# Float64 weights as twice their float32 by an integer addition, its steps spread over nine units of the attention

## The chip, the cores and the metric

The kernel runs on one core of one Trainium2 chip. The metric is the device time of one execution in microseconds (us). The core has TensorE (PE, its weight loads PEld), VectorE (DVE), ScalarE (ACT), GpSimd (POOL) and SyncE (SP, which here only issues DMAs). Each engine works off its own queue in order, so an instruction that waits holds back all that stand behind it on that engine.

## What is computed

```python
x = attention(q, k, v)          # 2 x 8 heads, 576 tokens, 64 wide, rotary; -> 1152 x 512
h = x @ w_in                    # w_in 512 x 2048, float64
x = (h / (1 + exp(-h))) @ w_out # w_out 2048 x 512, float64
out = 0
for e in range(4):              # w1[e] 512 x 1024, w2[e] 1024 x 512, float32
    out += p[:, e:e+1] * (relu(x @ w1[e]) @ w2[e])
```

q, k, v, w1 and w2 are float32. `w_in` and `w_out` come as float64, and no engine reads float64: each word is seen as two 32-bit integers, the low half `lw` and the high half `hw`, and must be turned into float32 on the chip. All large products are made with a high and a low part of each operand (`wh` and `wl` for weights: `wh` is the weight rounded to TensorE's fp32r, `wl` the rest), three matmuls for each product.

## The kernel before, in words

The attention works on 8 pairs of heads, each pair in 9 **units** (`P.units`: a block of 128 query rows of one head; the ninth takes the last 64 rows of both heads). `allu` holds the 72 units; the loop `for i, (P, un)` runs over them, `s = i % 9` is the unit's place in its pair. A unit's scores (`s`, L402 and on) go to PSUM, VectorE takes the row maximum (`nm`, L421), ScalarE the exponential (`p`, L431), TensorE transposes `p` into PSUM (L307), ScalarE copies the high part out (`pth`, L469) and VectorE the low part (`ptl`, L474), and later units multiply these by V (`b`, L507). `tmp` and `xu` (L517, L519) put the two halves of such a product together, `xn` (L560) normalizes, and `xh`, `xl` (L555, L556) are its split on ScalarE and GpSimd. The strings `ORDER` give the order of these steps inside each unit by hand, the lists `PLAN` the extra work of a unit; GpSimd rotates the next pair's keys and queries (L236 to L273) and splits its V (L290).

The conversion of the float64 weights is spread between them. `widen` (L83) makes the steps for one slice of 512 columns; a class `Feed` holds slices that wait, and `feed.tick(i in CONV)` at the end of every unit first runs one step of each slice under way and then, if the unit is in `CONV`, starts another, which issues its load (`raw0`, L1029, on SP) at once. In the attention four slices (unit 0 of `units`) are converted, with the steps of `slow=True`: four units in a row. They start at units 15, 24, 33 and 51 (later entries find nothing to start, but for 69). The other 28 slices (three steps each) are converted behind the attention, during the product with `w_in` and `w_out` (L645 to L675), while TensorE works; then come the experts (`l1r`, `Quartet`, `l2b`). One slice takes, before:

```python
ACT  t  = |hw| as float32                          # L90
DVE  lw = lw >> 9;  lw = hw << 23 | lw             # L91, L94
DVE  t  = max(t, 2**-15);  t = t << 3 & 0x3FFFF000 # L97, L100
DVE  t  = hw & 0xC0000000 | t                      # L103
ACT  wh = t                                        # L106
DVE  hw = t & 0xFF800000;  wl = lw * 2**-43 * hw   # L109, L112
```

Of the kernel before, what the change touches and what calls it, by code (L numbers as in the profile page):

```python
# [7 lines left out]
F32 = mybir.dt.float32  # L8
F32R = mybir.dt.float32r
U32 = mybir.dt.uint32  # L10
AF = mybir.ActivationFunctionType
ALU = mybir.AluOpType
# [5 lines left out]
ORDER = ['TvHSMEXVBL', 'SvTEBHVXML', 'vSTHEVMXBL', 'vSEVTBMXHL', 'THEvSVXMBL', 'vSVETHXMBL', 'vVSTEHMLXB', 'vTHSXLBEMV', 'vTSEXHVMBL']  # L18
ORDER0 = ['ETSHXMvVBL', 'TSEHXvVMBL', 'TSEHXMvVBL', 'TSXvEHMVBL', 'TXvVESHMBL', 'SEXVMTvHBL', 'SXMvVTEHLB', 'XESvMTVHBL', 'STvXEMHVBL']
ORDER2 = ['vSTEHLXVMB', 'vTVHSEXLMB', 'SvVEXTHMLB', 'vSEXMTHBVL', 'vTSVEXHMLB', 'vEVSTMXHBL', 'VETvSXHMLB', 'TvSVHEXMLB', 'vSMVTXEBHL']  # L20
CONV = [15, 24, 33, 51, 58, 61, 69]
DELAY = 2
RB1 = 0
RB0 = 4
# [7 lines left out]
def f32(ap):  # L32
    return ap.bitcast(F32)
# [3 lines left out]
def fused_kernel(ctx, tc, q, k, v, w_in, w_out, dprobs, w1, w2, cst, out):  # L37
    nc = tc.nc
# [7 lines left out]
    pers = ctx.enter_context(tc.tile_pool(name="pers", bufs=1))  # L46
# [16 lines left out]
    def new_slot(pool, i):  # L63
        wslot[i] = (
            pool.tile([128, FT, 512], F32R, name=f"wh{i}"),
            pool.tile([128, FT, 512], F32R, name=f"wl{i}"),
        )

    new_slot(pers, 0)

    w_in = w_in.bitcast(U32).rearrange("d (f a) -> d f a", a=2)
    w_out = w_out.bitcast(U32).rearrange("f (d a) -> f d a", a=2)
# [10 lines left out]
    def widen(cv, raw, wh, wl, slow=False):  # L83
        lw, hw = (raw.rearrange("p (n a) -> p n a", a=2)[:, :, a] for a in range(2))
        T = {}
        V = nc.vector

        def t0():
            T["t"] = t = cv.tile([128, 512], U32, name="cvt")
            nc.scalar.activation(f32(t), f32(hw), AF.Abs)  # L90
            V.tensor_scalar(lw, lw, 9, None, ALU.logical_shift_right)  # L91

        def t1():
            V.scalar_tensor_tensor(lw, hw, 23, lw, ALU.logical_shift_left, ALU.bitwise_or)  # L94

        def t2():
            V.tensor_scalar(f32(T["t"]), f32(T["t"]), 2.0 ** -15, None, ALU.max)  # L97

        def t3():
            V.tensor_scalar(T["t"][:], T["t"][:], 3, 0x3FFFF000, ALU.logical_shift_left, ALU.bitwise_and)  # L100

        def t4():
            V.scalar_tensor_tensor(T["t"][:], hw, 0xC0000000, T["t"][:], ALU.bitwise_and, ALU.bitwise_or)  # L103

        def t5():
            nc.scalar.copy(wh, f32(T["t"]))  # L106

        def t6():
            V.tensor_scalar(hw, T["t"][:], 0xFF800000, None, ALU.bitwise_and)  # L109

        def t7():
            V.scalar_tensor_tensor(wl, lw, 2.0 ** -43, f32(hw), ALU.mult, ALU.mult)  # L112

        def together(*fns):
            return lambda: [fn() for fn in fns]

        if slow:
            return [together(t0, t1), together(t2, t3, t4), t5, together(t6, t7)]
        return [together(t0, t1), together(t2, t3, t4), together(t5, t6, t7)]

    class Feed:
        def __init__(self):
# [46 lines left out]
    def bank(n, tag="b"):  # L169
        t = ps1.tile([128, 512], F32, tag=tag, name=tag)  # L170
        return t[:, 0:n]
# [422 lines left out]
    def flush(items):  # L594
        todo = list(items)
        items.clear()
        for e in todo:
            e()
# [27 lines left out]
    def mbank():  # L626
        psM.append(psM.pop(0))
        return psM[-1].tile([128, 512], F32, name="m")
# [3 lines left out]
    def l1(c, f, nb):  # L632
        if nb == 0:
            gt[c, f] = (
                gp.tile([128, NT], F32R, name="gh"),
                gp.tile([128, NT], F32R, name="gl"),
            )
        gh, gl = gt[c, f]
        wh, wl = wslot[(2 * c) % 4]
        ps = mbank()  # L640
        o = ps[:, 0:NB]
        cols = slice(nb * NB, (nb + 1) * NB)
        fs = slice(f * 128, (f + 1) * 128)
        for d in range(4):
            nc.tensor.matmul(o, wh[:, d, fs], xh[d][:, cols], start=(d == 0), stop=False)  # L645
            nc.tensor.matmul(o, wh[:, d, fs], xl[d][:, cols], start=False, stop=False)  # L646
            nc.tensor.matmul(o, wl[:, d, fs], xh[d][:, cols], start=False, stop=(d == 3))  # L647
        hi, lo = gh[:, cols], gl[:, cols]
        th = ep.tile([128, NB], F32, name="th")
        g2 = ep.tile([128, NB], F32, name="g2")  # L650
        nc.scalar.activation(th[:], o, AF.Tanh, scale=0.5)
        nc.vector.scalar_tensor_tensor(g2[:], th[:], 1.0, o, ALU.add, ALU.mult)
        flush(held)

        def split():
            nc.scalar.copy(hi, g2[:])  # L656
            (nc.gpsimd if c and nb < 2 else nc.vector).tensor_tensor(lo, g2[:], f32(hi), ALU.subtract)  # L657

        held.append(split)
# [20 lines left out]
    def xsplit(src, dst, cols):  # L680

        hi, lo = (t[cols] for t in dst)
        return [lambda: nc.scalar.activation(hi, src, AF.Copy, scale=0.5),
                lambda: nc.vector.scalar_tensor_tensor(lo, src, 0.5, f32(hi), ALU.mult, ALU.subtract)]

    def xforms(j):

# [38 lines left out]
    def wforms(raw):  # L726

        q = {x: raw[:, 2 * dh:2 * dh + 2, 256 * fh:256 * fh + 256]
             for x, dh, fh in (("a", 0, 0), ("b", 1, 0), ("c", 0, 1), ("d", 1, 1))}
        T = {}  # L730

        def task(name, add=None):
            hi, lo = wf[name]

            def s0():
                if add:
                    x, y, op = add
                    T[name] = cv.tile([128, 512], U32, name="cvt")
                    t = f32(T[name]).rearrange("p (k f) -> p k f", k=2)
                    nc.vector.tensor_tensor(t, src(x), src(y), op)  # L740
                nc.scalar.copy(hi, src(name))  # L741

            def s1():
                nc.gpsimd.tensor_tensor(lo, src(name), f32(hi), ALU.subtract)  # L744

            return [s0, s1]

        def src(x):
            return f32(T[x]).rearrange("p (k f) -> p k f", k=2) if x in T else q[x]

        return [lambda: task("a"), lambda: task("b"), lambda: task("s1", ("c", "d", ALU.add)),
                lambda: task("s2", ("s1", "a", ALU.subtract)), lambda: task("s4", ("b", "s2", ALU.subtract)),
                lambda: task("s3", ("c", "a", ALU.subtract)), lambda: task("d")]
# [151 lines left out]
    def moe():  # L905
# [5 lines left out]
        for c in range(NC1):  # L911
# [81 lines left out]
    def attention():  # L993
# [26 lines left out]
        nc.scalar.dma_start(cs[:, 1280:NCST], cst[:, 1280:NCST])  # L1020
        idle = xp.tile([128, 128], F32, name="idle")
        nc.vector.memset(idle[:], 0.0)
        spin = bank(128)
        for i in range(NWARM):
            nc.tensor.matmul(spin, idle[:], idle[:], start=True, stop=True)

        def slice0(t):
            raw = stg0.tile([128, 1024], U32, name="raw0")
            nc.sync.dma_start(raw[:], units[0][:, t, :])  # L1029
            return widen(cv0, raw, wslot[0][0][:, t, :], wslot[0][1][:, t, :], True)  # L1030
# [118 lines left out]
        for i, (P, un) in enumerate(allu):  # L1149
# [67 lines left out]
            while gq and (s == 8 or left > gq[0][0] / 2):  # L1217
                c, fn = gq.pop(0)
                fn()
                left -= c  # L1220
            feed.tick(i in CONV)
            if i == 9 * (NPAIR - 1) - 1:
                feed.need(0)
                lctx.close()
                s1 = ctx.enter_context(tc.tile_pool(name="s1", bufs=1))
                stg = ctx.enter_context(tc.tile_pool(name="stg", bufs=2))
                cv = ctx.enter_context(tc.tile_pool(name="cv", bufs=3))
                new_slot(s1, 1)
                queue(1)
        flush(lows)  # L1230
# [7 lines left out]
        rbc(P, 1)  # L1238
        feed.need(0)
        l1(0, 0, 0)  # L1240
        run(av(P, 1, 0))
        run(av(P, 1, 1))
        evac()
        l1(0, 1, 0)
        feed.tick(True)
        run(norm(P, 1))
# [8 lines left out]
    with tc.manual_schedule():  # L1255
        attention()
# [70 lines left out]
```

## Time and profile before

| | |
|---|---|
| median of 3 runs | 767.4 us (767.36 to 767.52) |
| the profiled execution, its own time | 767.15 us |
| its span, first to last instruction | 765.0 us |
| busy: PE, PEld, DVE, ACT, POOL | 744.6, 693.9, 509.7, 341.5, 286.4 us |
| granted TensorE clock, mean | 0.998 of full speed |

The span is what lies between the first and the last instruction; 2.15 us lie around it. The attention fills the first 177 us, the product with the float64 weights some 175 us behind it, the experts the rest. PE's busy time counts pipelined matmuls, so in a stretch where it is as long as the stretch, the matmuls follow each other without a gap; where it falls short, they wait for something.

### The profile page before, as it was taken

The numbers are of one execution on the slowest core, as the hardware profiler recorded it, in microseconds if no ns is written. First come the engines' busy times: TensorE is split into PE (matmuls) and PEld (weight loads), VectorE is DVE, ScalarE is ACT, GpSimd is POOL, SyncE is SP. The second block draws the span as 40 slices with busy tenths as digits, with TensorE's granted clock in tenths as the row PEclk, the third lists the DMA queues.
The fourth block names the chain that finished last, engine by engine and source line by source line (L and its number), as shares of the span: only waits on it lengthen the run. The fifth ranks groups of instructions, "written<-read, shape, count | busy, mean of one in ns | idle before, by whom it ended". The sixth has DMA issues, their size and how long they took to land.

```text
span 765.0 us, 11981 instructions
## 1 busy us (share of the span) xinstructions
PE 744.6 (97%) x4546; PEld 693.9 (91%) x4546; DVE 509.7 (67%) x936; ACT 341.5 (45%) x806; POOL 286.4 (37%) x310
## 2 busy tenths in 40 slices
PE   7899889999999999999999999999999999999998
PEld 6888879899999999999998898989989899898996
DVE  6789998987999899895565454545445454454542
ACT  5788888885533525325223242423314233141330
POOL 8987777421001303105341703416043261422600
PEclk9999999999999999999999999999999999999999
DMA  4455434230313133131110110301103020020002
GB/s 130 120 133 127 125 89 116 58 124 2 111 56 111 56 110 111 56 111 56 56 56 0 56 56 1 111 1 58 54 0 111 1 86 25 22 90 1 0 28 97
DMA packets 31129, 51.88 MB, mean 68 GB/s; under 512 B 7184, under 2 KB 14112, under 8 KB 31072
## 3 DMA queue, kind: packets, MB, share of 16 engines
q1 hardware_dynamic: 28720, 50.05, 21.3%
q10 hardware_dynamic: 2224, 0.79, 0.4%
q8 instruction: 36, 0.59, 0.3%
q0 software_dynamic: 128, 0.28, 0.1%
q14 instruction: 21, 0.17, 0.1%
HBM read 41.40 MB, written 2.36 MB: 57 GB/s over the span
## 4 chain that ended last, share of the span: by engine, by line
PE 65%; DVE 6%; ACT 0%; issue 0%; POOL 0%
PE m L834 9%; PE m L835 9%; PE m L836 9%; PE m L761 7%; PE m L763 7%; PE m L762 7%; PE m L670 3%; PE m L668 3%; PE m L669 3%; PE m L647 2%; PE m L645 2%; PE m L646 2%; PE m L718 1%; PE m L720 1%; PE m L719 1%; DVE cvt L103 1%
## 5 line engine op out<-in xcount | busy, mean ns | idle before, releaser
L840 DVE SCALAR_TENSOR_TENSOR acc<-m,dp,acc 128x512 f32<-128x512 f32 (+1 forms) x64 | 47.5, 742 | 108.3 <-PE m L836 108.3
L835 PE MATMUL m<-wl,gh 128*128 128x512 f32 (+1 forms) x292 | 113.2, 388 | 0.0
L834 PE MATMUL m<-wh,gh 128*128 128x512 f32 (+1 forms) x292 | 113.1, 387 | 0.0
L836 PE MATMUL m<-wh,gl 128*128 128x512 f32 (+1 forms) x292 | 112.7, 386 | 0.0
L782 DVE SCALAR_TENSOR_TENSOR gl<-g,gh 128x288 fp32r<-128x288 f32 x84 | 51.0, 607 | 44.6 <-ACT gh L781 43.3
L744 POOL TENSOR_TENSOR wl<-raw,wh 128x512 fp32r<-128x512 f32 x21 | 27.2, 1295 | 141.6 <-ACT wh L741 141.6
L657 POOL TENSOR_TENSOR gl<-g,gh 128x384 fp32r<-128x384 f32 x24 | 26.8, 1120 | 141.3 <-ACT gh L656 112.8
L761 PE MATMUL m<-xh,wh 128*128 128x288 f32 x224 | 66.1, 295 | 0.0
L763 PE MATMUL m<-xh,wl 128*128 128x288 f32 x224 | 66.0, 295 | 0.0
L762 PE MATMUL m<-xl,wh 128*128 128x288 f32 x224 | 65.9, 294 | 0.0
L836 PEld LDWEIGHTS m<-wh,gl 128*128 128x128 f32 x292 | 54.9, 188 | 11.4
L834 PEld LDWEIGHTS m<-wh,gh 128*128 128x128 f32 x292 | 54.8, 188 | 10.7
L670 PE MATMUL m<-gl,wh 128*128 128x384 f32 x192 | 64.2, 335 | 0.1
L835 PEld LDWEIGHTS m<-wl,gh 128*128 128x128 f32 x292 | 54.8, 188 | 10.3
L669 PE MATMUL m<-gh,wl 128*128 128x384 f32 x192 | 64.1, 334 | 0.0
L668 PE MATMUL m<-gh,wh 128*128 128x384 f32 x192 | 64.1, 334 | 0.0
L744 POOL TENSOR_TENSOR wl<-cvt,wh 128x512 fp32r<-128x512 f32 x28 | 36.2, 1293 | 69.7 <-ACT wh L741 69.7
L421 DVE TENSOR_REDUCE nm<-s 128x1 f32<-128x576 f32 x72 | 53.9, 748 | 9.3 <-PE s L402 5.4
L741 ACT CAST wh<-cvt 128x512 fp32r<-128x512 f32 x28 | 17.4, 621 | 89.4 <-DVE cvt L740 89.4
L431 ACT ACTIVATE p<-s,nm 128x576 f32<-128x576 f32 x72 | 54.0, 750 | 5.2 <-DVE nm L421 4.6
L307 PE MATMUL b<-cs,p 128*128 128x128 f32 x329 | 49.7, 279 | 6.7 <-DVE xn L560 1.8
L474 DVE TENSOR_TENSOR ptl<-b,pth 128x512 fp32r<-128x512 f32 x72 | 48.8, 685 | 5.3 <-ACT pth L469 4.1
(180 smaller groups left out, 2107.7 us busy)
## 6 DMA issues: line engine op xcount, KB each, us to landing
raw<-in_moe_w_dram SPq DMA_DIRECT2D x16, 1024.0 KB, 5.1
raw<-in_moe_w_out_dram SPq DMA_DIRECT2D x8, 1024.0 KB, 4.9
raw<-in_moe_w_in_dram SPq DMA_DIRECT2D x6, 1024.0 KB, 5.2
kh<-kkh SPq DMA_DIRECT2D x28, 128.0 KB, 2.3
kl<-kkl SPq DMA_DIRECT2D x28, 128.0 KB, 2.3
xv<-in_v_dram SPq DMA_DIRECT2D x8, 256.0 KB, 2.7
raw<-in_moe_w_in_dram SPq DMA_DIRECT2D x4, 512.0 KB, 3.9
xk<-in_k_dram SPq DMA_DIRECT2D x7, 256.0 KB, 2.9
```

What stands on the lines that cost most here:

```text
L421: nc.vector.tensor_reduce(P.nm[:, c:c + 1], s[:, :, 0:288], AX.XY, ALU.max, negate=True)
L431: nc.scalar.activation(o.rearrange("p (a b) -> p a b", a=2), s[:, :, 0:288], AF.Exp, bias=P.nm[:, c:c + 1], scale=1.0, accum_out=P.sm[:, c ...
L668: nc.tensor.matmul(o, wh[:, f, ds], gh[:, cols], start=(f == 0), stop=False)
L669: nc.tensor.matmul(o, wl[:, f, ds], gh[:, cols], start=False, stop=False)
L670: nc.tensor.matmul(o, wh[:, f, ds], gl[:, cols], start=False, stop=(f == FT - 1))
L744: nc.gpsimd.tensor_tensor(lo, src(name), f32(hi), ALU.subtract)
L761: nc.tensor.matmul(ps, wh[:, k, ms], hh[:, k, cols], start=(first and k == 0), stop=False, skip_group_check=not first)
L762: nc.tensor.matmul(ps, wh[:, k, ms], hl[:, k, cols], start=False, stop=False, skip_group_check=not first)
L763: nc.tensor.matmul(ps, wl[:, k, ms], hh[:, k, cols], start=False, stop=(k == 1), skip_group_check=not first)
L834: nc.tensor.matmul(ps, gh[:, ts], wh[:, f, ds], start=(f == 0), stop=False)
L835: nc.tensor.matmul(ps, gh[:, ts], wl[:, f, ds], start=False, stop=False)
L836: nc.tensor.matmul(ps, gl[:, ts], wh[:, f, ds], start=False, stop=(f == FT - 1))
```

## The change

The weight becomes twice its float32 by one 32-bit integer addition. ScalarE makes, beside `t`, a word `y = lw * 2**-29 + 2**23` as an integer: the 2**23 raises the exponent of the float32 by one (hence twice the weight), the rest are the three mantissa bits that come from `lw`, rounded. VectorE prepares `t` as before and adds `y`; ScalarE copies `wh`, and the low part is `t - wh`, now on GpSimd. The steps for one slice, after:

```python
ACT  t  = |hw|;  y = lw * 2**-29 + 2**23           # L92, L93
DVE  t  = max(t, 2**-15);  t = t << 3 & 0x3FFFFFF8 # L97, L98
DVE  t  = hw & 0xC0000000 | t                      # L101
DVE  t  = t + y, integers                          # L104
ACT  wh = t                                        # L107
POOL wl = t - wh                                   # L108
```

```diff
-CONV = [15, 24, 33, 51, 58, 61, 69]
+CONV = [18, 27, 36, 45, 69]
...
+    big = pers.tile([128, 32], F32, name="big")
...
         def t0():
-            T["t"] = t = cv.tile([128, 512], U32, name="cvt")
-            nc.scalar.activation(f32(t), f32(hw), AF.Abs)
-            V.tensor_scalar(lw, lw, 9, None, ALU.logical_shift_right)
+            T["t"] = cv.tile([128, 512], U32, name="cvt", tag="cv")
+            T["y"] = cv.tile([128, 512], U32, name="cvy", tag="cv")
+            nc.scalar.activation(f32(T["t"]), f32(hw), AF.Abs)
+            nc.scalar.activation(T["y"][:], lw, AF.Identity, scale=2.0 ** -29, bias=big[:, 0:1])
 
         def t1():
-            V.scalar_tensor_tensor(lw, hw, 23, lw, ALU.logical_shift_left, ALU.bitwise_or)
+            t = T["t"]
+            V.tensor_scalar(f32(t), f32(t), 2.0 ** -15, None, ALU.max)
+            V.tensor_scalar(t[:], t[:], 3, 0x3FFFFFF8, ALU.logical_shift_left, ALU.bitwise_and)
 
         def t2():
-            V.tensor_scalar(f32(T["t"]), f32(T["t"]), 2.0 ** -15, None, ALU.max)
+            V.scalar_tensor_tensor(T["t"][:], hw, 0xC0000000, T["t"][:], ALU.bitwise_and, ALU.bitwise_or)
 
         def t3():
-            V.tensor_scalar(T["t"][:], T["t"][:], 3, 0x3FFFF000, ALU.logical_shift_left, ALU.bitwise_and)
+            V.tensor_tensor(T["t"][:], T["t"][:], T["y"][:], ALU.add)
 
         def t4():
-            V.scalar_tensor_tensor(T["t"][:], hw, 0xC0000000, T["t"][:], ALU.bitwise_and, ALU.bitwise_or)
-
-        def t5():
             nc.scalar.copy(wh, f32(T["t"]))
-
-        def t6():
-            V.tensor_scalar(hw, T["t"][:], 0xFF800000, None, ALU.bitwise_and)
-
-        def t7():
-            V.scalar_tensor_tensor(wl, lw, 2.0 ** -43, f32(hw), ALU.mult, ALU.mult)
+            G.tensor_tensor(wl, f32(T["t"]), f32(wh), ALU.subtract)
...
         if slow:
-            return [together(t0, t1), together(t2, t3, t4), t5, together(t6, t7)]
-        return [together(t0, t1), together(t2, t3, t4), together(t5, t6, t7)]
+            rest = together()
+            return [t0, rest, t1, rest, rest, t2, t3, rest, t4]
+        return [t0, together(t1, t2, t3), t4]
```

What follows from the doubled weights is in constants alone: the scale of the tanh (0.5 to 0.25) and of `xsplit` (0.5 to 0.125). `big` is filled once at the start, and the pool `cv` of the second phase has 4 buffers for 3. The load of a slice moves with `CONV`: the slices start at units 18, 27, 36 and 45, the first unit of pairs 2 to 5, and their nine steps (four of them empty) end in the first unit of the next pair.

How that moves instructions is shown at three places. The first is the start of a pair, on SP and on ACT. SP's queue holds the loads of V for a later pair (`xv`), the copies of the transposed keys to the other half of the partitions (`kh`, `kl`) and the slice's load (`raw`). Before, from pair 1 on:

```order
L205 DMA xk<-in_k_dram 64x64 x2
L1029 DMA raw_1420<-in_moe_w_in_dram 128x1024
L200 DMA xq<-in_q_dram 128x2x256
L205 DMA xq<-in_q_dram 64x64 x2
L222 DMA v_0_114<-in_v_dram 64x64 x2
L211 DMA xv<-in_v_dram 128x2x256
L322 DMA kh_119<-kkh 64x512 x4
L322 DMA kl_121<-kkl 64x512 x4
```

and of the change:

```order
L202 DMA xk<-in_k_dram 64x64 x2
L197 DMA xq<-in_q_dram 128x2x256
L202 DMA xq<-in_q_dram 64x64 x2
L219 DMA v_1_116<-in_v_dram 64x64 x2
L208 DMA xv<-in_v_dram 128x2x256
L1027 DMA raw_1858<-in_moe_w_in_dram 128x1024
L319 DMA kh_119<-kkh 64x512 x4
L319 DMA kl_121<-kkl 64x512 x4
```

The slice's load now stands right behind `xv` and ahead of the eight key copies. On ScalarE, units 1 and 2 of the pair, before:

```order
L469 CAST pth<-b 128x4x128
L471 COPY p_1189<-b 128x128
L555 CAST xh<-xn 128x256
L469 CAST pth<-b 128x4x128
L431 ACTIVATE p,sm_113<-s,nm 128x576
L354 ACTIVATE Q<-b 128x512
L517 COPY tmp<-b 64x320
```

and of the change:

```order
L466 CAST pth<-b 128x4x128
L468 COPY p_1180<-b 128x128
L552 CAST xh<-xn 128x256
L92 ACTIVATE cvt<-raw_1222 128x512
L93 ACTIVATE cvy<-raw_1222,big 128x512
L466 CAST pth<-b 128x4x128
L428 ACTIVATE p,sm_114<-s,nm 128x576
L351 ACTIVATE Q<-b 128x512
L514 COPY tmp<-b 64x320
```

Both of the slice's first ScalarE instructions now stand ahead of the copy of unit 2's transposes. The second place is VectorE in units 3 and 4. Before:

```order
L474 TENSOR_TENSOR ptl<-b,pth 128x4x128
L483 TENSOR_REDUCE rs<-sm_113 128x4
L485 RECIPROCAL rs<-rs 128x4
L560 TENSOR_TENSOR xn<-xu,b 128x320
L421 TENSOR_REDUCE nm<-s 128x1
```

and of the change:

```order
L471 TENSOR_TENSOR ptl<-b,pth 128x4x128
L480 TENSOR_REDUCE rs<-sm_114 128x4
L482 RECIPROCAL rs<-rs 128x4
L97 TENSOR_SCALAR cvt<-cvt 128x512
L98 TENSOR_SCALAR cvt<-cvt 128x512
L557 TENSOR_TENSOR xn<-xu,b 128x320
L418 TENSOR_REDUCE nm<-s 128x1
```

The two steps with one input now stand ahead of `xn` and of a row maximum. The third place is VectorE in units 6 to 8. Before:

```order
L421 TENSOR_REDUCE nm<-s 128x1
L474 TENSOR_TENSOR ptl<-b,pth 128x4x128 x2
L421 TENSOR_REDUCE nm<-s 128x1
L91 TENSOR_SCALAR raw_1420<-raw_1420 128x512
L94 SCALAR_TENSOR_TENSOR raw_1420<-raw_1420 128x512
L519 TENSOR_TENSOR xu<-b,tmp 64x256
```

and of the change:

```order
L471 TENSOR_TENSOR ptl<-b,pth 128x4x128
L101 SCALAR_TENSOR_TENSOR cvt<-raw_1222,cvt 128x512
L471 TENSOR_TENSOR ptl<-b,pth 128x4x128
L418 TENSOR_REDUCE nm<-s 128x1
L104 ISA cvt<-cvt,cvy 128x1024
L516 TENSOR_TENSOR xu<-b,tmp 64x256
```

The OR now stands between the `ptl` of units 6 and 7, and the addition, printed as an instruction of its own kind over 1024 elements, behind the maximum. The three steps that stood behind unit 8's reciprocal (L97, L100, L103) and the two behind unit 1's `ptl` (L109, L112) are gone from those places.

## Rows read from the trace of the kernel before

**Rows 1.** Busy time by stretch: start:end, length, PE, PEld, DVE, ACT, POOL busy, PEclk.

```profile
49.98:73.03 23.05, 20.20 (x149) 18.04 (x148) 22.12 (x38) 18.57 (x48) 17.81 (x20) 1.00 0.46 120
73.03:95.23 22.20, 20.21 (x149) 18.04 (x148) 21.30 (x38) 18.43 (x49) 16.58 (x19) 1.00 0.44 113
95.23:117.43 22.20, 20.20 (x148) 18.02 (x147) 21.31 (x38) 18.43 (x48) 16.56 (x19) 1.00 0.36 87
117.43:137.33 19.90, 19.59 (x149) 18.13 (x148) 15.94 (x31) 17.13 (x48) 15.46 (x20) 1.00 0.39 109
137.33:159.16 21.83, 20.30 (x152) 18.31 (x151) 20.42 (x38) 18.76 (x51) 6.52 (x10) 1.00 0.27 63
...
195.00:350.00 155.00, 154.93 (x894) 154.60 (x893) 143.76 (x283) 64.31 (x130) 22.66 (x20) 1.00 0.29 96
350.00:763.00 413.00, 411.24 (x2389) 376.99 (x2388) 201.11 (x358) 125.84 (x288) 138.01 (x126) 1.00 0.13 42
```

**Rows 2.** Waits of PEld: instruction, what it waited for, us in total, times, longest.

```profile
PEld m L670 <- POOL gl L657: 0.4, 1, 0.4
```

**Rows 3.** Groups by line and form, whole run: count, busy us, mean ns, idle before.

```profile
L103 DVE SCALAR_TENSOR_TENSOR cvt<-raw,cvt 128x512 uint32<-128x512 uint32 x32 | 23.7, 741 | 1.1
L94 DVE SCALAR_TENSOR_TENSOR raw<-raw 128x512 uint32<-128x512 uint32 x32 | 23.3, 728 | 1.1
...
L97 DVE TENSOR_SCALAR cvt<-cvt 128x512 f32<-128x512 f32 x32 | 15.4, 482 | 0.0
...
L100 DVE TENSOR_SCALAR cvt<-cvt 128x512 uint32<-128x512 uint32 x32 | 14.0, 437 | 1.1
```

**Rows 4.** The page's groups: GpSimd's subtraction of 128x512, in the experts.

```profile
L744 POOL TENSOR_TENSOR wl<-cvt,wh 128x512 fp32r<-128x512 f32 x28 | 36.2, 1293 | 69.7 <-ACT wh L741 69.7
```

**Rows 5.** Timeline of SP in pair 5: start us, us, instruction.

```profile
122.96 0.37 SPq L211 DMA_DIRECT2D xv<-in_v_dram  x1
123.45 1.12 SPq L322 DMA_DIRECT2D kh<-kkh  x2
```

**Rows 6.** DMA issues: count, KB each, median us to landing.

```profile
raw<-in_moe_w_in_dram SPq DMA_DIRECT2D x4, 512.0 KB, 3.9
```

**Rows 7.** Timeline of ACT, pair 5 and the start of pair 6: idle before in brackets.

```profile
126.09 0.43 ACT L555 CAST xh<-xn 128x256 fp32r<-128x256 f32 x1
126.89 0.59 ACT L469 CAST pth<-b 128x512 fp32r<-128x512 f32 x1 [0.37 <-PE b L307]
...
129.03 0.42 ACT L517 COPY tmp<-b 64x320 f32<-64x320 f32 x1 [0.34 <-PE b L507]
129.47 0.74 ACT L431 ACTIVATE p<-s,nm 128x576 f32<-128x576 f32 x1
...
132.26 0.55 ACT L555 CAST xh<-xn 128x256 fp32r<-128x256 f32 x2
...
138.05 0.69 ACT L90 ACTIVATE cvt<-raw 128x512 f32<-128x512 f32 x1
138.60 0.62 ACT L354 ACTIVATE Q<-b 128x512 fp32r<-128x512 f32 x1
```

**Rows 8.** Timeline of DVE in pair 5, which converts nothing.

```profile
118.14 0.75 DVE L421 TENSOR_REDUCE nm<-s 128x1 f32<-128x576 f32 x1
119.71 0.43 DVE L519 TENSOR_TENSOR xu<-b,tmp 64x256 f32<-64x256 f32 x1 [0.81 <-ACT tmp L517]
120.74 0.76 DVE L421 TENSOR_REDUCE nm<-s 128x1 f32<-128x576 f32 x1 [0.60 <-PE s L402]
...
131.70 0.46 DVE L560 TENSOR_TENSOR xn<-xu,b 128x320 f32<-128x320 f32 x1
```

**Rows 9.** Timeline of POOL around 52 us, pair 2.

```profile
52.05 1.46 POOL L273 TENSOR_TENSOR yq<-t,yq 128x576 f32<-128x576 f32 x1
```

**Rows 10.** Timeline of DVE at the same time.

```profile
52.28 1.78 DVE L94 SCALAR_TENSOR_TENSOR raw<-raw 128x512 uint32<-128x512 uint32 x1
```

More of the change, by code (lines that the diff above doesn't have):

```diff
@@ L85, in widen @@
         T = {}
-        V = nc.vector
+        V, G = nc.vector, nc.gpsimd
         def t0():
-            T["t"] = t = cv.tile([128, 512], U32, name="cvt")
-            nc.scalar.activation(f32(t), f32(hw), AF.Abs)
-            V.tensor_scalar(lw, lw, 9, None, ALU.logical_shift_right)
+            T["t"] = cv.tile([128, 512], U32, name="cvt", tag="cv")
+            T["y"] = cv.tile([128, 512], U32, name="cvy", tag="cv")
+            nc.scalar.activation(f32(T["t"]), f32(hw), AF.Abs)
+            nc.scalar.activation(T["y"][:], lw, AF.Identity, scale=2.0 ** -29, bias=big[:, 0:1])
         def t1():
-            V.scalar_tensor_tensor(lw, hw, 23, lw, ALU.logical_shift_left, ALU.bitwise_or)
+            t = T["t"]
+            V.tensor_scalar(f32(t), f32(t), 2.0 ** -15, None, ALU.max)
+            V.tensor_scalar(t[:], t[:], 3, 0x3FFFFFF8, ALU.logical_shift_left, ALU.bitwise_and)
         def t2():
-            V.tensor_scalar(f32(T["t"]), f32(T["t"]), 2.0 ** -15, None, ALU.max)
+            V.scalar_tensor_tensor(T["t"][:], hw, 0xC0000000, T["t"][:], ALU.bitwise_and, ALU.bitwise_or)
         def t3():
-            V.tensor_scalar(T["t"][:], T["t"][:], 3, 0x3FFFF000, ALU.logical_shift_left, ALU.bitwise_and)
+            V.tensor_tensor(T["t"][:], T["t"][:], T["y"][:], ALU.add)
         def t4():
-            V.scalar_tensor_tensor(T["t"][:], hw, 0xC0000000, T["t"][:], ALU.bitwise_and, ALU.bitwise_or)
-        def t5():
             nc.scalar.copy(wh, f32(T["t"]))
-        def t6():
-            V.tensor_scalar(hw, T["t"][:], 0xFF800000, None, ALU.bitwise_and)
-        def t7():
-            V.scalar_tensor_tensor(wl, lw, 2.0 ** -43, f32(hw), ALU.mult, ALU.mult)
+            G.tensor_tensor(wl, f32(T["t"]), f32(wh), ALU.subtract)
         def together(*fns):
@@ L650, in l1 @@
         g2 = ep.tile([128, NB], F32, name="g2")
-        nc.scalar.activation(th[:], o, AF.Tanh, scale=0.5)
+        nc.scalar.activation(th[:], o, AF.Tanh, scale=0.25)
         nc.vector.scalar_tensor_tensor(g2[:], th[:], 1.0, o, ALU.add, ALU.mult)
@@ L682, in xsplit @@
         hi, lo = (t[cols] for t in dst)
-        return [lambda: nc.scalar.activation(hi, src, AF.Copy, scale=0.5),
-                lambda: nc.vector.scalar_tensor_tensor(lo, src, 0.5, f32(hi), ALU.mult, ALU.subtract)]
+        return [lambda: nc.scalar.activation(hi, src, AF.Copy, scale=0.125),
+                lambda: nc.vector.scalar_tensor_tensor(lo, src, 0.125, f32(hi), ALU.mult, ALU.subtract)]
     def xforms(j):
@@ L737, in s0 @@
                     x, y, op = add
-                    T[name] = cv.tile([128, 512], U32, name="cvt")
+                    T[name] = cv.tile([128, 512], U32, name="cvt", tag="cv")
                     t = f32(T[name]).rearrange("p (k f) -> p k f", k=2)
@@ L1022, in attention @@
         nc.vector.memset(idle[:], 0.0)
+        nc.vector.memset(big[:], 2.0 ** 23)
         spin = bank(128)
@@ L1226, in attention @@
                 stg = ctx.enter_context(tc.tile_pool(name="stg", bufs=2))
-                cv = ctx.enter_context(tc.tile_pool(name="cv", bufs=3))
+                cv = ctx.enter_context(tc.tile_pool(name="cv", bufs=4))
                 new_slot(s1, 1)
```

## Prediction

> **What bounds the kernel now.** I read the busy times by stretch first, to see where time can be won at all. From 195 us to the end of the experts PE is busy as long as the stretch: 154.93 of 155.00 us, and 411.24 of 413.00 [rows 1]. A full PE goes no faster because another engine has less to do, so the 28 slices that are converted there bring nothing, whatever VectorE saves. The one wait in that part that the wait list shows is 0.4 us, a matmul behind a low part `gl` on GpSimd, at a place where VectorE is behind with its work [rows 2].
>
> That leaves the attention. The rows by stretch are cut at the exponentials of units 17, 26, 35 and so on, one row for nine units, so each row is about one pair's work [rows 1]. PE is not full in any of them. The row from 117.43 to 137.33 holds no conversion and takes 19.90 us. The three before it hold one slice each and take 23.05, 22.20 and 22.20, the one behind it (pair 6, fewer GpSimd steps) holds the fourth slice and takes 21.83. In the converted pairs VectorE is busy 21.3 of 22.2 us, without conversion 15.94 of 19.90: it is the bound only where it converts, and a slice puts some 5.4 us (21.31 - 15.94) on it. So an attention slice costs 3.15, 2.30 and 2.30 us of time, where the pair without one is the measure. The fourth has no such pair beside it; between nothing and 2.30 I take 1.9, near the others' price, lower because GpSimd, which lengthens VectorE's steps (below), is busy there only 6.52 us against 16.56 [rows 1]. In all the four slices cost 9.65 us now. That is what can be won, and only if the new slices cost nothing.
>
> **What the change does to a pair.** Four pairs carry a slice as before, but pair 5 gets one and pair 6 loses its own, so the sum is 4 times the new price of a slice against 9.65. I go through the new steps in the order of the pair without conversion, whose rows show where its engines have room.
>
> *Start, ScalarE.* The load of the slice stands behind `xv` on SP. `xv` went out at 122.96 and the next DMA at 123.45 [rows 5]; a load of this size takes 3.9 us to land [rows 6], so the data is there at 127.35. ScalarE comes to its first conversion step when `xh` is done, at 126.09 + 0.43 = 126.52 [rows 7]: it waits 0.8 us for the DMA, and everything behind it on ScalarE waits too. Then come two instructions. The absolute value takes 0.69 us and lets the next one start 0.55 us later (138.05 to 138.60) [rows 7]. The new one, which makes `y`, is in no row; its bounds are 0.59 (a copy of 512 columns) and 0.74 (an exponential of 576 columns with a per-partition bias) [rows 7], and I take 0.6 from start to start, like its neighbour, which reads the same strided words. The copy `pth` of unit 2 then starts at 127.35 + 0.55 + 0.6 = 128.5 where it started at 126.89: 1.6 us late. Behind it ScalarE had 0.34 us idle in front of `tmp` [rows 7]; the rest, 1.2 us, reaches the exponential at 129.47 and, since ScalarE has no idle time in the rows that follow up to 132.26, the scores and row maxima that wait for it.
>
> By the Trainium skill, page "ScalarE: Activation LUTs", section "What ACT_TABLE_LOAD costs", a bias read per partition makes an ACTIVATE some 93 ns longer than a constant one. No row shows the pair side by side; by that rule the sum below would be 0.4 us larger (an estimate, four slices).
>
> *The maximum and the shift, VectorE.* These take 0.48 + 0.44 = 0.92 us [rows 3] in front of `xn`, which ended at 131.70 + 0.46 = 132.16 [rows 8]. ScalarE's `xh` took it at 132.26 [rows 7] and stands there ahead of `tmp` and an exponential, so only 0.1 us is room and 0.8 us goes on to the pair. It adds to the 1.2, since VectorE comes to this place through ScalarE's `pth`, which is already late.
>
> *The OR and the addition, VectorE.* The OR takes 0.74 [rows 3]. The addition is in no row. Its low bound is 0.44, the cheapest step over 512 columns, its high bound twice a two-input step, 1.48, because it counts 1024 elements [rows 3]. I take 0.7: it moves the same bytes as a two-input step over 512 words, the nearest rows. Around here VectorE has 0.81 us idle in front of `xu` and 0.60 in front of the next maximum [rows 8]: 1.41 of room for 1.44 of work. I take nothing.
>
> Here a page matters. By the Trainium skill, page "VectorE: DVE Perf Modes", section "What auto-detection actually checks", the engine handles two results a cycle when all tensors are 16 bits wide with step one, if firmware enables the mode for the instruction. By that, 1024 halves cost as much as 512 words, about 0.7 us; without it twice that, which is the second rival below.
>
> *End.* The copy `wh` (as before) lies in ScalarE's idle time in front of a `tmp`, and the subtraction on GpSimd takes 1.29 us [rows 4], where GpSimd stands idle for its own `xl`. I take nothing for either; without that cover it would be up to 1.3 us on GpSimd, and the rotation, which nobody awaits before the next pair, would be late. The fill of `big` lies in the start, beside loads; the tanh and `xsplit` constants change no duration.
>
> So a new slice costs 1.2 + 0.8 = 2.0 us, four of them 8.0 against 9.65. Add 0.3 for the wait of 0.4 us in the product, which a lighter VectorE should shorten. The profiled execution took 767.15 us (span 765.0), so it would take 767.15 - 1.65 - 0.3 = 765.2. The median of the runs stands 0.25 higher: **765.4 us**, 0.26% below before. VectorE loses half of its conversion work, and most of that is given back to ScalarE.
>
> **The rivals.** *ScalarE's part is hidden.* If the exponentials have more slack than I see, or the load comes sooner, only the 0.8 us of the maximum and shift stays: 3.2 against 9.65, and 760.7 us. For it: VectorE, the present bound, drops to about 18.5 of 19.9 us in a pair. Against it: ScalarE rises from 17.13 busy [rows 1] by 0.69, 0.7 and 0.6 to 19.1 in 19.9, and a queue that full is rarely hidden.
>
> *The addition runs at one element a cycle* (slower). It then takes some 1.4 us instead of 0.7, and the room of 1.41 is already used up. GpSimd makes it worse: VectorE's steps with two SBUF inputs and GpSimd's instructions hold each other up, as when a step of 0.73 on average [rows 3] took 1.78 us beside GpSimd's own 1.46 [rows 9, 10]; the addition stands beside the same GpSimd line, L273. With 0.7 and 0.3 more a slice costs 3.0, four 12.0: 769.4 us. It decides from 2.5 us a slice: beyond that the kernel is slower than before.
>
> *The subtractions hold up the product* (slower). The 28 low parts `wl` go into GpSimd's queue with the `gl` of the same product. If three of the changes from one product to the next each find a 1.29 us subtraction in front of the `gl` that the matmul needs, that is 3.9 us: 769.3. Against it: GpSimd is busy 22.66 of 155 us there [rows 1], 59 with them.
>
> **How the numbers follow.** The forecast (a slice at 1.6 to 2.5 us) gets 0.53, the hidden ScalarE 0.25, the long addition 0.16, the late subtractions 0.06. A measurement of this kernel tells about 0.2%, 1.5 us. Faster by more than that, below 765.9, needs a slice under 2.1: the first rival and a bit more than half of the forecast, 0.55. Within 0.2% is the rest of the forecast, 0.24. Slower by more than 0.2% are the last two with a little of the slice prices between: 0.21. The range goes from the first rival's 760.7 to the second's 769.4, with a little at either end, and leaves out 0.2.
>
> **What would show it.** Right: the four stretches of 19.9 and 22 us each near 21.9, pair 6 near 20, the product unchanged; ScalarE's first conversion step ends an idle time on a DMA of `raw`, 0.5 us or more in each pair; VectorE busy below 19 us in each pair. The first is wrong if ScalarE does not wait for `raw`, or if the pairs come out at 20.7 (first rival). The addition's duration settles the second rival: 0.7 or 1.4 us. A wait of PE for `gl` or `wl` in the product would show the third. I would be wrong altogether if PE's stretches behind 195 us change length.

## The result, and the profile after

The changed kernel takes **773.73 us** (median of four, 771.39 to 774.15) against 767.38 before: ratio 1.0079, 95% interval 1.0067 to 1.0091. It is slower by 0.8%; the forecast was 765.4 with a range of 760.5 to 769.5. The execution that was profiled is the quickest of the four, 771.39 us (span 769.6), so its trace can show 4.2 of the 6.3 us that were lost. The other executions have a lower granted clock, 0.995 to 0.991 against 0.997. One execution of a later kernel (`max_unit_earlier`, 1243.33 us at a clock of 0.601) is slow as a whole and is left out of that kernel's figures.

Busy time by stretch, after, cut at the exponentials of the same units (columns as in [rows 1]):

```profile
49.94:72.43 22.49, 20.08 (x149) 17.97 (x148) 16.66 (x33) 18.37 (x48) 16.44 (x20) 1.00 0.42 113
72.43:95.60 23.17, 20.16 (x149) 17.97 (x148) 18.24 (x35) 18.88 (x49) 16.70 (x20) 1.00 0.40 112
95.60:118.10 22.50, 20.17 (x149) 17.94 (x148) 18.24 (x35) 18.89 (x50) 16.68 (x20) 1.00 0.36 106
118.10:140.58 22.48, 20.17 (x149) 17.95 (x148) 18.25 (x35) 18.97 (x50) 16.82 (x21) 1.00 0.33 96
140.58:160.85 20.27, 19.86 (x152) 18.39 (x151) 17.57 (x33) 17.95 (x50) 7.85 (x11) 1.00 0.29 68
...
195.00:350.00 155.00, 152.98 (x878) 152.34 (x878) 120.25 (x199) 75.84 (x147) 52.34 (x43) 1.00 0.28 91
```

VectorE went from 21.3 to 18.25 us in a pair, as forecast, and yet the five stretches take 110.91 us where they took 109.18: 1.7 us lost in the attention. Against five pairs at the 19.90 us of the one without a slice, a slice now costs (110.91 - 99.50) / 4 = 2.85 us, where the forecast had 2.0 and before 2.4. And PE is no longer full in the product: 152.98 of 155 us, against 154.93 [rows 1].

What the attention waits for stands in the wait list of 49 to 141 us (us in total, times, longest), and the DMA issues of the page (count, KB each, us to landing):

```profile
PE s L399 <- ACT p L428: 7.9, 8, 2.2
ACT cvt L92 <- DMA raw<-in_moe_w_in_dram: 6.4, 4, 2.1
```

```profile
kh<-kkh SPq DMA_DIRECT2D x28, 128.0 KB, 3.8
...
raw<-in_moe_w_in_dram SPq DMA_DIRECT2D x4, 512.0 KB, 4.6
```

ScalarE waits 1.6 us for every slice's load, twice the 0.8 of the forecast, because the load takes 4.6 us to land there and not the 3.9 of [rows 6]. It now travels together with `xv`, `kh` and `kl`; the copies of `kh`, which landed in 2.3 us before, take 3.8 as well. One such place, on ScalarE and then on PE:

```profile
58.58 0.43 ACT L552 CAST xh<-xn 128x256 fp32r<-128x256 f32 x1
60.60 0.67 ACT L92 ACTIVATE cvt<-raw 128x512 f32<-128x512 f32 x1 [1.59 <-DMA raw<-in_moe_w_in_dram]
61.18 0.74 ACT L93 ACTIVATE cvy<-raw,big 128x512 uint32<-128x512 uint32 x1
61.83 0.56 ACT L466 CAST pth<-b 128x512 fp32r<-128x512 f32 x1
62.29 0.73 ACT L428 ACTIVATE p<-s,nm 128x576 f32<-128x576 f32 x1
```

```profile
63.17 0.53 PE L399 MATMUL s<-kh,Q 128*128 128x288 f32 x2 [1.68 <-ACT p L428]
```

The exponential stands behind both conversion steps, and PE is idle for 1.68 us until it is done. In the product PE stalls at one place, 261 to 265 us, in the first `w_out` matmuls of the second chunk. PE, and the three engines that make its operands (start, length, idle before in brackets):

```profile
262.99 0.44 PE L665 MATMUL m<-gh,wh 128*128 128x384 f32 x1 [1.06 <-ACT gh L653]
...
264.57 0.45 PE L667 MATMUL m<-gl,wh 128*128 128x384 f32 x1 [0.96 <-POOL gl L654]
```

```profile
258.31 1.27 DVE L97 TENSOR_SCALAR cvt<-cvt 128x512 f32<-128x512 f32 x1
259.62 0.43 DVE L98 TENSOR_SCALAR cvt<-cvt 128x512 uint32<-128x512 uint32 x1
260.08 0.69 DVE L101 SCALAR_TENSOR_TENSOR cvt<-raw,cvt 128x512 uint32<-128x512 uint32 x1
260.81 0.69 DVE L104 CUSTOM_DVE_ANT_0 cvt<-cvt,cvy 128x1024 uint16<-128x1024 uint16 x1
```

```profile
261.53 0.62 ACT L107 CAST wh<-cvt 128x512 fp32r<-128x512 f32 x1 [2.54 <-DVE cvt L104]
262.06 0.49 ACT L648 ACTIVATE th<-m 128x384 f32<-128x384 f32 x1
262.44 0.50 ACT L653 CAST gh<-g 128x384 fp32r<-128x384 f32 x1
```

```profile
258.28 1.02 POOL L654 TENSOR_TENSOR gl<-g,gh 128x384 fp32r<-128x384 f32 x1 [0.59 <-ACT gh L653]
262.23 1.33 POOL L108 TENSOR_TENSOR wl<-cvt,wh 128x512 fp32r<-128x512 f32 x1 [2.92 <-ACT wh L107]
263.53 1.97 POOL L654 TENSOR_TENSOR gl<-g,gh 128x384 fp32r<-128x384 f32 x2
```

The four VectorE steps stand in one block, which takes 3.2 us, 0.9 of it because the maximum takes 1.27 us beside a GpSimd instruction (0.41 at 220.90 us, where GpSimd stands idle). ScalarE's copy `wh` waits 2.54 us for the block, with `th` and `gh` behind it; GpSimd then does `wl` ahead of `gl`. Both operands are late, where one had been 0.4 us late [rows 2].

The product has a second loss, and it is no stall. Two blocks of 144 `w_in` matmuls, whose weights the trace names `tf`, follow each other more slowly though PE is never idle in them. First and last start of the first block, before and then after:

```profile
233.17 0.33 PE L645 MATMUL m<-xh,tf 128*128 128x384 f32 x1
257.95 0.33 PE L647 MATMUL m<-xh,tf 128*128 128x384 f32 x1
```

```profile
234.86 0.34 PE L642 MATMUL m<-xh,tf 128*128 128x384 f32 x1
260.03 0.34 PE L644 MATMUL m<-xh,tf 128*128 128x384 f32 x1
```

That is 24.78 us before and 25.17 after. The second block takes 24.79 and 25.17, so the two lose 0.8 us together. Every other run of this study shows 25.17, also those that convert the product's weights in the old steps, so the steps are not the reason. The reason stays open.

The new steps themselves, by line and form over the whole run (count, busy us, mean ns):

```profile
L97 DVE TENSOR_SCALAR cvt<-cvt 128x512 f32<-128x512 f32 x32 | 24.4, 762 | 3.8 <-ACT cvt L92 3.8
...
L93 ACT ACTIVATE cvy<-raw,big 128x512 uint32<-128x512 uint32 x32 | 24.0, 749 | 0.9 <-POOL wl L108 0.9
L104 DVE CUSTOM_DVE_ANT_0 cvt<-cvt,cvy 128x1024 uint16<-128x1024 uint16 x32 | 22.8, 712 | 2.7
L92 ACT ACTIVATE cvt<-raw 128x512 f32<-128x512 f32 x32 | 21.3, 667 | 6.4 <-DMA raw<-in_moe_w_in_dram 6.4
```

The addition takes 0.71 us on average, as assumed; the maximum 0.76 where it took 0.48 [rows 3].

### The profile page after: what moved, and what is told of

It is laid out like the page before. It is cut to its first block, busy times and chain, and to the rows that moved or that the text cites. A ratio compares the mean times of both kernels' runs of the same rounds, so it can differ in the third digit from the quotient of the medians.

```text
span 769.6 us, 11999 instructions
## 1 busy us (share of the span) xinstructions
PE 746.5 (97%) x4546; PEld 695.2 (90%) x4546; DVE 474.1 (62%) x841; ACT 360.2 (47%) x838; POOL 322.5 (42%) x342
## 4 chain that ended last, share of the span: by engine, by line
PE 84%; ACT 5%; POOL 3%; DMA 3%; DVE 3%; issue 1%; POOLq 0%; ACTq 0%; SPq 0%
PE m L831 9%; PE m L832 9%; PE m L833 9%; PE m L759 7%; PE m L758 7%; PE m L760 7%; PE m L667 4%; PE m L665 4%; PE m L666 4%; PE m L642 4%; PE m L644 4%; PE m L643 4%; PE b L504 3%; PE b L304 3%; DMA raw<-in_moe_w_in_dram 2%; ACT p L428 2%
## 5 line engine op out<-in xcount | busy, mean ns | idle before, releaser
L741 POOL TENSOR_TENSOR wl<-cvt,wh 128x512 fp32r<-128x512 f32 x28 | 36.3, 1295 | 69.6 <-ACT wh L738 69.6
L667 PE MATMUL m<-gl,wh 128*128 128x384 f32 x192 | 64.3, 335 | 1.0 <-POOL gl L654 1.0
L108 POOL TENSOR_TENSOR wl<-cvt,wh 128x512 fp32r<-128x512 f32 x24 | 31.6, 1317 | 65.8 <-ACT wh L107 65.8
```

The lines of the kernel that those rows point to most:

```text
L667: nc.tensor.matmul(o, wh[:, f, ds], gl[:, cols], start=False, stop=(f == FT - 1))
```

## The experiments

**Which half loses.** Two kernels take one half of the change each. `widen_before` is the old function with twice the weights (the copy `wh` gets a scale of 2, the last step 2^-42), so that the other constants of the change stay.

```diff
 def widen(cv, raw, wh, wl, slow=False):      # att_new_prod_old
+    if not slow:
+        return widen_before(cv, raw, wh, wl, slow)
```
```diff
-CONV = [18, 27, 36, 45, 69]                  # att_old_prod_new
+CONV = [15, 24, 33, 51, 58, 61, 69]
 def widen(cv, raw, wh, wl, slow=False):
+    if slow:
+        return widen_before(cv, raw, wh, wl, slow)
```

> The four slices of the attention are converted as in the change; the 28 of the product (and w_out's first unit) as before, with twice the weights from a scale in the copy and 2^-42 in the last step. Theory 1 (the product's share of the loss is the stall of PE at the start of the second w_out product of chunk 1, from the new conversion, and the lower granted clock of the other executions follows that stall): 767.4 + 1.7 of the attention = 769.1 us, no stall at 261 us, granted clock 0.997 or more in every execution. Rival (the lower clock comes from the attention's gaps): 769.1 + 2.3 = 771.4, clock 0.991 to 0.995 in most executions.

Measured: 769.67 us (768.65 to 770.93), ratio 1.0035 (1.0022 to 1.0047). The two quickest, 768.7, are 1.5 above before. The stall at 261 us is gone, but the clock did not stay up: the profiled execution (770.93 us) has a stretch at half clock from 132.68 to 136.09, behind a PE that stood idle for 1.96 us (the first line):

```profile
131.73 0.53 PE L439 MATMUL s<-kh,Q 128*128 128x288 f32 x2 [1.96 <-ACT p L468]
132.68:136.09 3.41, 3.41 (x18) 3.41 (x17) 3.26 (x9) 2.56 (x7) 0.12 (x1) 0.50 0.00 1
```

> The four slices of the attention are converted as before and in the units of before; the product's 28 as in the change. Theory 1: 767.4 + 2.9 (stall) + 2.3 (clock) = 772.6 us, stalls behind ACT gh and POOL gl as in the change, clock 0.991 to 0.995 in most executions. Rival (clock from the attention's gaps): 767.4 + 2.9 = 770.3 at 0.997. If the product is not the place: 767.4.

Measured: 771.0 us (769.31 to 771.15), ratio 1.0046 (1.0034 to 1.0059). The profiled execution, at 769.31 with clock 0.998, shows the two stalls, 2.1 us over before; the other four are at 0.995 and 1.5 to 1.8 us slower. So both halves lose, 1.5 and 2.1 us, and each figure holds the 0.8 us of the `w_in` matmuls. For the first half the trace shows a fall of the clock behind a gap of the attention, as the rival said; for the second the four slower executions left no trace, and their lower clock is only a sign. An execution's mean clock tells little by itself: in the first kernel 770.82 us, as slow as the profiled one, stands at 0.998.

**The load.** `load_early` issues each slice's load two units earlier and leaves the steps where they are.

```diff
-CONV = [18, 27, 36, 45, 69]
+CONV = [16, 25, 34, 43, 69]
-return [t0, rest, t1, rest, rest, t2, t3, rest, t4]
+return [rest, rest, t0, rest, t1, rest, rest, t2, t3, rest, t4]
```

> The change with the load of each slice issued two units earlier, so that it no longer stands behind xv; every conversion step stays in its unit. Theory 2 (ScalarE's wait for the load, 1.6 us in each of four pairs, goes through to the pair): the waits of L92 for DMA are gone, pairs of 21.2 to 21.7 instead of 22.5, 4 to 5 us less in all: 768.7 to 769.7. Rival (a slice costs its ScalarE, VectorE and lock time wherever the load stands): the waits go, pairs stay at 22.3 or more, 773 us.

Measured: 764.72 us (764.26 to 768.43), ratio 0.9981 (0.9969 to 0.9993): 0.2% quicker than before the change. The waits of L92 are gone, the load lands in 3.9 us and `kh` in 2.4 again:

```profile
49.91:70.72 20.81, 20.12 (x149) 18.01 (x148) 16.67 (x33) 18.25 (x48) 16.34 (x20) 1.00 0.38 101
70.72:91.73 21.01, 20.17 (x148) 17.96 (x147) 18.25 (x35) 18.79 (x49) 16.69 (x20) 1.00 0.45 119
91.73:112.72 20.99, 20.13 (x148) 17.93 (x147) 18.24 (x35) 18.79 (x49) 16.70 (x20) 1.00 0.46 118
112.72:133.81 21.09, 20.19 (x149) 17.99 (x148) 18.24 (x35) 18.86 (x50) 16.86 (x21) 1.00 0.41 106
133.81:154.09 20.28, 19.86 (x152) 18.38 (x151) 17.58 (x33) 17.92 (x49) 7.87 (x11) 1.00 0.28 67
```

All engines are as busy as in the changed kernel, and the five stretches take 104.18 us instead of 110.91: 1.68 us a slice, the whole of the wait (1.6) and a little more. (The slower `kh` is not behind it: no engine waits for a DMA of `kh` in the changed kernel's list of 49 to 141 us.) A slice's price is then 1.17 us. Theory 2 holds, and the gain is larger than it expected. The profiled executions alone give the same: 771.39 against 764.72.

**The product's stall.** `wl_vector` takes the 28 subtractions off GpSimd:

```diff
-G.tensor_tensor(wl, f32(T["t"]), f32(wh), ALU.subtract)
+(G if slow else V).tensor_tensor(wl, f32(T["t"]), f32(wh), ALU.subtract)
```

> The change with the product's 28 subtractions wl on VectorE instead of GpSimd; the attention unchanged. Theory 1a (half of the stall at 261 us is gl standing behind wl on GpSimd, 1.1 us; the other half is ScalarE's copy wh that waits for VectorE): stall 1.2 instead of 2.4, 772.6 us, or 770.3 if the clock then stays at 0.997. Rival (only the wh copy behind VectorE's block counts, and VectorE gets longer by 28 steps of 0.55 to 0.7): stall 2.4 or more, 773.7 to 776.

Measured: 771.66 us (769.97 to 772.39). PE's waits are 0.6 for `gh` and 0.5 for `gl` instead of 1.1 and 1.0: about half of the stall is left, as expected, but both halves shrank, not the one behind `gl` alone. The clock was 0.995 in four of five executions; the slowest, 772.39, has 0.998. The next three start from `load_early`.

```diff
-return [t0, together(t1, t2, t3), t4]        # early_prod_stages
+return [t0, t1, together(t2, t3), t4]
```
```diff
-nc.scalar.copy(wh, f32(T["t"]))              # early_wh_vector, in the product
+nc.vector.tensor_copy(wh, f32(T["t"]))
```

> load_early with the product's 28 slices converted as before (twice the weights by a scale in the copy and 2^-42 in the last step). Theory 1 (the product's loss is the stall at the start of the second w_out product of chunk 1, and nothing else there): 764.7 - 2.1 to 2.4 = 762.3 to 762.6 us, no stall above 0.5 us near 255 us, granted clock 0.997 in nearly all executions. Rival (the product's new conversion saves elsewhere what it loses there): 764 or more.

> load_early with the product's conversion in four steps instead of three (maximum and shift one step ahead of OR and addition). Theory 1b (the stall comes from one uninterrupted block of four VectorE steps, 3.1 us, that the copy wh and all of ScalarE behind it wait for): the block is 1.4 us, the stall falls from 2.4 to 1.2 us or less, 762.4 to 763.5. Rival (the work counts, not the block: VectorE and GpSimd lengthen each other wherever the steps stand): stall 2 us or more, 764.7.

> load_early with the product's 28 copies wh on VectorE instead of ScalarE, so that ScalarE's queue holds no instruction that waits for the conversion. Theory 1c (the gh half of the stall is ScalarE standing in that wait): the 1.2 us behind gh goes, the 1.1 behind gl stays or shrinks: 763.5 us. Rival (g itself stands behind the block on VectorE, now 0.4 us longer): stall 2.4 or more, 764.7 to 766.

Measured: `early_prod_old` (with the `if not slow` of above) 762.12 us (762.07 to 762.59), 2.6 less than `load_early`; `early_prod_stages` 762.63 (762.51 to 763.0), 2.1 less, with neither `gh` nor `gl` in PE's waits in the product. All new steps are still there on the same engines; the block on VectorE is cut in two, and with that the copy `wh` and the subtraction come one step later, behind one `gl` more on GpSimd. So the stall came from how the steps stand together, not from their number; the length of the block and the later place of `wh` and `wl` were not tested apart. `early_wh_vector` missed: 766.8 us (764.97 to 768.14). PE's wait for `gh` in the matmuls' own rows went, but the one for `gl` grew to 2.0 us, and the clock fell to 0.50 behind it, from 258.90 to 262.31 us (L670 in this kernel is L667 in the changed one):

```profile
258.36 0.44 PE L670 MATMUL m<-gl,wh 128*128 128x384 f32 x1 [1.97 <-POOL gl L657]
```

ScalarE's wait alone was not the cause; freeing it moved the delay to the other operand.

**What is left of a slice.** Three kernels leave out one piece of the attention's slices each, from `early_prod_stages` (762.63).

> early_prod_stages with one part left out: in the attention's four slices ScalarE doesn't make y (the addition adds a tile of zeros, so the low bits of these weights are missing). The prediction's step (the second ScalarE instruction puts its 0.6 us on each pair): 4 x 0.6 less, 762.6 - 2.4 = 760.2 us, pairs near 20.4. Rival (once the load no longer keeps it waiting, ScalarE has room for it): 762.2 or more, pairs 20.9 to 21.1.

> early_prod_stages with one part left out: in the attention's four slices the maximum and the shift are not done (these weights come out wrong). The prediction's step (ahead of xn these 0.82 us of VectorE put 0.8 us on each pair): 4 x 0.8 less, 759.4 us, pairs near 20.2. Rival (they stand in room there, too): 762 or more.

> early_prod_stages with one part left out: in the attention's four slices the OR and the addition are not done (these weights come out wrong). The prediction's step (1.44 us of work in 1.41 us of room, nothing on the pair): 762.6 us, pairs 20.9 to 21.1. Rival (the OR stretched to 1.02 us by GpSimd beside it, with the addition's 0.68, is what is left of a slice's price): up to 1.0 us less a pair, 758.6.

Measured: 761.74 us (761.62 to 762.2) without `y`, 759.73 (759.69 to 760.03) without maximum and shift, 761.95 (761.61 to 762.26) without OR and addition. That is 0.9, 2.9 and 0.7 us for four slices: 0.22, 0.72 and 0.17 a slice, together 1.1 of 1.17. With the load early, `y` is nearly hidden, the maximum and shift cost what was forecast.

**Where maximum and shift stand.** Moved to the unit of the OR (`early_max_late`, from `load_early`), one unit earlier or one later (both from `early_prod_stages`):

```diff
-[rest, rest, t0, rest, t1, rest, rest, t2, t3, rest, t4]
+[rest, rest, t0, rest, rest, rest, rest, together(t1, t2), t3, rest, t4]  # early_max_late
+[rest, rest, t0, t1, rest, rest, rest, t2, t3, rest, t4]                  # max_unit_earlier
+[rest, rest, t0, rest, rest, t1, rest, t2, t3, rest, t4]                  # max_unit_later
```

> load_early with the attention's maximum and shift taken from ahead of xn to the unit of the OR, so that three of the four VectorE steps stand together. The prediction's step (maximum and shift ahead of xn put 0.8 us on each of four pairs, while the other place has room): 764.7 - 3.2 = 761.5 us, pairs near 20.2. Rival (the room there is filled by OR and addition, 1.44 of 1.41 us, so that 0.9 us more there go to the pair as well): pairs at 20.8 to 21.2, 764 to 765.5 us.

> early_prod_stages with the attention's maximum and shift one unit earlier, so that they no longer stand between the reciprocal and xn. If their price (0.67 us a pair by no_max_shift) is the place: VectorE has 0.8 to 1.0 us idle ahead of ptl and xu there, pairs of 20.3 to 20.5, 4 x 0.6 = 2.4 less: 760.2 us. Rival (0.82 us of VectorE work cost the pair that much wherever they stand): pairs at 20.9 to 21.1, 762.6.

> early_prod_stages with the attention's maximum and shift one unit later, behind xn and ahead of ScalarE's next wait. If the place counts and only xn's is bad: 760.2 to 761 us. Rival (the following unit's row maxima wait for them just as xn did, as in early_max_late): 762.6 to 766.

Measured: 775.41 us (771.06 to 775.79), 763.8 (763.43 to 763.93) and 761.5 (761.43 to 761.58). The first is 10.7 us slower than `load_early`, far beyond its rival. VectorE, GpSimd and ScalarE there:

```profile
93.16 1.52 DVE L98 TENSOR_SCALAR cvt<-cvt 128x512 uint32<-128x512 uint32 x1
94.72 0.69 DVE L101 SCALAR_TENSOR_TENSOR cvt<-raw,cvt 128x512 uint32<-128x512 uint32 x1
```
```profile
92.93 1.47 POOL L270 TENSOR_TENSOR yq<-t,yq 128x576 f32<-128x576 f32 x1
```
```profile
96.77 0.74 ACT L428 ACTIVATE p<-s,nm 128x576 f32<-128x576 f32 x1 [2.04 <-DVE nm L418]
```

The shift takes 1.52 us beside GpSimd's L270 instead of 0.43, the next row maximum is late, the exponential waits 2.04 us and PE stalls again in each pair, with the clock at half behind the last of these (143.54 to 146.95). One unit earlier the shift meets another GpSimd step (L241) and takes 1.53 us: no gain, 1.2 us slower. One unit later is 1.1 us less, and not for quicker steps. `early_prod_stages`, where the two meet no GpSimd step, and then `max_unit_later`, where they do:

```profile
64.51 0.40 DVE L97 TENSOR_SCALAR cvt<-cvt 128x512 f32<-128x512 f32 x1
64.94 0.43 DVE L98 TENSOR_SCALAR cvt<-cvt 128x512 uint32<-128x512 uint32 x1
```
```profile
66.17 0.62 DVE L97 TENSOR_SCALAR cvt<-cvt 128x512 f32<-128x512 f32 x1
66.83 0.51 DVE L98 TENSOR_SCALAR cvt<-cvt 128x512 uint32<-128x512 uint32 x1
```

What goes is ScalarE's wait for `xn`. This line of the wait list of `early_prod_stages` (49 to 155 us: in total, times, longest) is not in that of `max_unit_later`:

```profile
ACT xh L552 <- DVE xn L557: 2.5, 4, 0.6
```

So place decides, by two things: what waits behind the steps on VectorE, and whether GpSimd runs a long step beside them. By the Trainium skill, page "GPSIMD Engine Reference", section "Key points", GpSimd shares its SBUF interfaces with VectorE and collides with VectorE instructions that run in a two-port mode or read two SBUF inputs. The trace agrees for the OR: 0.69 us alone, 1.02 beside L267 and L270. That the shift, which reads one input, is hit harder would fit the two-port mode, but no run here shows an instruction's mode.

`max_unit_later` is the quickest kernel of the study that does all the work: ratio 0.9922 (0.9910 to 0.9935) against the kernel before.

**The missing 2.3 us.** The changed kernel once more:

> The changed kernel itself once more. Theory (its time lies above the 771.4 of the profiled execution because the granted clock falls to half for 3.4 us at a time behind a stall of PE, and how often differs between executions): the executions order by granted clock, some 770.7 to 771.4 at 0.997 and 1.5 to 2.8 us more at 0.995 to 0.991; if the profiled one is among the latter, the fall lies within 3 us behind one of the five stalls (four pairs, 262 us). Rival (something else varies): times do not follow the clock, or the fall stands elsewhere.

Measured: 772.51 us (770.26 to 776.1). The six executions: 770.26 at clock 0.997, 771.7 at 0.996, 772.38 at 0.995, 772.64 and 774.87 at 0.993, 776.1 at 0.991. The last is the profiled one. Its stretches around the first and the last of its three falls (PEclk is the last column but two):

```profile
61.75:64.03 2.28, 0.30 (x3) 0.30 (x3) 0.69 (x1) 2.28 (x6) 2.19 (x3) 1.00 0.82 200
64.03:67.44 3.41, 3.41 (x18) 3.39 (x18) 2.31 (x6) 2.14 (x6) 0.76 (x1) 0.50 0.22 69
...
265.00:268.83 3.83, 1.94 (x10) 1.40 (x9) 2.87 (x5) 3.62 (x8) 3.26 (x3) 1.00 0.00 0
268.83:272.24 3.41, 3.41 (x13) 3.41 (x12) 1.27 (x3) 0.03 (x1) 0.00 (x0) 0.50 0.00 0
```

Each time PE had been idle for 1.9 to 2.55 us, twice behind the exponential and once, in two parts, at the product's stall; then the granted clock stands at 0.50, 1.2 GHz, while PE is full. Over all profiled executions such a fall was seen six times behind 30 us and ahead of the end, each 0.3 to 1.2 us behind a stall's end. It doesn't follow every stall: the first profile of the changed kernel has five and no fall. In the kernels without a PE gap above 1 us (`early_prod_old`, `early_prod_stages`, `max_unit_later`) no fall was seen, and the executions of each lie within 0.6 us.

The order by clock holds for the changed kernel but not for all. In `wl_vector` the profiled execution has 0.995, is the quickest of its five, and shows no fall behind 30 us; its lower mean comes from the start, where a stretch at half clock lasts 6.83 us, against 3.41 (10.17 to 13.58) in the changed kernel's first profile:

```profile
9.34:16.17 6.83, 6.11 (x26) 5.49 (x27) 4.50 (x8) 3.78 (x10) 6.25 (x12) 0.50 0.10 34
```

A mean clock of 0.995 is thus no proof of a fall. Only a trace shows one, and the executions that were not profiled left none.

## Why the prediction was wrong

The bill for the profiled execution, from the starts of the same instructions before and after: 1.7 us in the attention, 2.2 at the stall in the product and 0.8 in the `w_in` matmuls make 4.7; the spans differ by 4.6, and 0.4 less lies outside the span, which leaves the 4.2 measured. The median lies 2.3 higher. The clock's falls are the likely cause and can be as large: in the slowest execution of `after_again` the matmuls around the third fall lose 1.5 us against the same ones of the first profile. For the executions behind the median it is not shown.

- **Old price, 9.65 us for four slices:** read from the trace before; no run tested it by itself.
- **The wait for the load, 0.8 us:** this term of the step "Start, ScalarE" was mis-sized. I took the landing time of a load that travelled nearly alone, 3.9 us, for one that I had just placed between `xv`, `kh` and `kl`. It was 4.6, the wait 1.6, and the pair paid 1.68. The 0.34 us of room in front of `tmp` absorbed nothing of it. (The sum was also short by itself: 128.50 - 126.89 - 0.34 is 1.27 and not 1.2.)
- **ScalarE's two steps:** too dear, as far as tested. With the load early, `y` costs 0.22 a slice, not 0.6; behind a late load it was not tested. By its duration I was wrong the other way (0.75). By the Trainium skill, page "ScalarE: Activation LUTs", section "What ACT_TABLE_LOAD costs", a per-partition bias costs some 93 ns. The trace about agrees: 0.75 against the absolute value's 0.67, 0.08 more, though the two write different types.
- **Maximum and shift, 0.8 on the pair:** right, 0.72, and for the forecast's reason (no room ahead of `xn`): behind `xn` they cost 0.3 less. The reason is only part of it; where GpSimd is long at work the same steps cost far more.
- **OR and addition, nothing:** nearly, 0.17. The addition takes 0.67 to 0.70 us in 31 of 32 places, so the second rival is out. By the Trainium skill, page "VectorE: DVE Perf Modes", section "What auto-detection actually checks", the engine handles two results a cycle when all tensors are 16 bits wide with step one, if firmware enables the mode for the instruction. The duration agrees, 1024 halves in the time of a two-input step over 512 words (0.69); no run shows the mode itself.
- **Product, -0.3:** this step failed. I wrote that a wait of 0.4 us would vanish because VectorE is lighter; instead the product lost 3.0 us, 2.2 of it at the stall. VectorE is lighter on the whole, 120 against 144 us of 155, but the conversion's steps became one chain: four on VectorE in a block, then ScalarE's `wh`, then GpSimd's `wl`, and on each queue the operands of the next matmuls stand behind. The third rival had the GpSimd part of this, at three boundaries and 3.9 us; it came at one, with ScalarE in it as well. The other 0.8 us, in the `w_in` matmuls, stood in no rival.
- **The sum against the median:** it had no term for the clock. I took PE's gaps in the attention for their length alone; behind some of them, 2.0 to 2.6 us long in the changed kernel, a stretch at half clock was seen.

Of what would show it right, "VectorE busy below 19 us" and "L92 waits for `raw`" came true, the pairs near 21.9 and the unchanged product did not.

## What to carry to other kernels

When steps move to an emptier engine, look at what stands behind them in that engine's queue and how long their inputs take to arrive at the new place, in the new company; the load here cost more than all the arithmetic, and issuing it two units earlier turned the loss into a gain. Cut a chain of conversion steps where it crosses engines, so that no queue waits for a block on another. A PE gap can cost more than its length: behind gaps of 1.1 to 2.6 us the granted clock fell to 0.50 in some executions, and one such fall made the product 1.5 us longer.

## What the runs showed that was not expected

A shift and mask of 512 words on VectorE, one input and two constants, took 0.43 us alone and 1.52 beside a GpSimd instruction of 1.47; the prediction had looked for this only at steps with two inputs. And the spread of a kernel's executions told something: the versions with PE stalls spread over 1.8 to 6 us, those without over 0.65 at most.
